# Loads of q and k by head group in a fused block-sparse attention and FFN kernel, with new instruction orders

## The chip, the cores and the metric

The kernel runs on one core of a Trainium2 chip. The metric is the device time of one execution in microseconds, the median of several runs. A profile is one execution recorded by the hardware profiler, with its own time. A core has the engines TensorE (PE), VectorE (DVE), ScalarE (ACT), GpSimd (POOL) and SyncE (SP); SP, ACT and POOL also issue DMAs, which 16 DMA engines carry out.

## The reference: what is computed

The inputs q, k and v have 4 batches, 8 heads, 768 positions and 64 dimensions, in float32. For every query, chunks of 32 keys are ranked by an upper bound of the score, the six best causal chunks are kept, and attention runs over them:

```python
k_chunks = k.reshape(B, H, nc, chunk, D)
k_min = np.min(k_chunks, axis=3)
k_max = np.max(k_chunks, axis=3)
ub = np.sum(np.maximum(q[:, :, :, None, :] * k_min[:, :, None, :, :], q[:, :, :, None, :] * k_max[:, :, None, :, :]), axis=-1)
ub = np.where(causal, ub, -1000000000.0)
top_chunks = np.argsort(ub, axis=-1)[..., -top_k:]
scores = scale * np.matmul(q, k.transpose(0, 1, 3, 2))
mask = sel & (pos[:, None] >= pos[None, :])
...
attn = attn / (np.sum(attn, axis=-1, keepdims=True) + 1e-09)
return np.matmul(attn, v).astype(np.float32)
```

The result, 3072 tokens by 512 features, goes through an RMS norm and a gated FFN:

```python
xn = x / rms * rms_g
g = xn @ w_gate
silu = g * (1.0 / (1.0 + np.exp(-g)))
return (silu * (xn @ w_val) @ w_out).astype(np.float32)
```

## The kernel before

**Blocks.** The tokens are cut into 12 blocks of 256, each a batch b and a third m of its sequence, in the order `ORDER` (line 340). Blocks 0, 1 and 2 of that order are (0,0), (1,0) and (2,0). The eight heads make two groups g of four heads a. In a tile with 128 partitions, partition 32a + r holds row r of head a.

**One block.** `load_qk` (line 423) issues the loads of q and k into `qraw` and `kraw`, `load_v` (451) those of v into `VX`, and `load_w` and `load_wo` those of the weights (`wg`, `wv`, `wo`, three pieces each). `job(i, g)` handles a group: VectorE transposes k and q in 32x32 squares (`turn k`, `turn q`, line 631), ACT or POOL casts them to bf16 (`half k`, `half q`), VectorE reduces the minima and maxima of the chunks (`ext0`, `ext1`), `dk` subtracts them, `bd0` and `bd1` lay them out for TensorE, and `relu` (725) takes the positive part of q over `qraw`. TensorE then forms the bounds (`upper`), VectorE makes the mask from them (`ubn`, `bar`, `top`, `mk`, `mt`, `swap`), TensorE computes the scores and adds the mask (`scores`, lines 751 and 762), ACT takes the exponential (`exp`, 801), POOL clears the triangle (`tri`, 771), TensorE multiplies by v (`values`, 827), and VectorE normalises (`rden`, `norm`). `norm` of a block (`square`, `rms`, `scale`, `turn`, `xsT`) is the RMS norm and the transpose for the FFN. The FFN has gate and value matmuls (`wg(i, tokens).h` and `wv(i, tokens).h`, line 951), an activation (`tanh`, `tg`, `vcopy`, `hh`) and the output projection (`project`, 998, which needs all of `wo`), then `out` and `store`.

**What sets the order.** Every operation is entered in a list with its readers and writers. `Plan.run` (227) then issues them in the order written in the table `STEPS`: entry e names operation e // 8 and, by e % 8, the engine that does it (0 PE, 1 ACT, 2 DVE, 3 POOL, 4 SP); a negative entry is a run of filler matmuls, which compute nothing that is used. `SLOTS` gives the buffer for each tile. Each engine does its instructions in this order and waits by semaphore for what it needs, so an operation also waits for all that stands ahead of it on its engine. The cost numbers in the code served the search for the order and do nothing at run time.

**Loads before.** In blocks 0 to 2 (`PACKED`) one DMA brings 32 rows of one head a for both groups, 128 KB, so k and q take four DMAs each. In block 0 they alternate between SP and ACT, in the others all are on SP. From block 3 on, a DMA brings one head of one group (64 KB). The first load of block 2 waits until the piece wg1 has landed, and the first of block 3 until wo0 has (`HELD`, 421). Weights and v are cast to bf16 on the way and come by POOL's queue. On POOL the order begins: constants, both v loads of block 0, wg0, `half k(0,0,0)`, wg1, `dk(0,0,0)`, wv0, wv1, both v loads of block 1, wg2, wv2, wo0, wo1, wo2, with small operations between them. On TensorE the first FFN matmul `wg(0,(0,)).0` stands ahead of `scores(1,0,1)0a` and `upper(1,0,1)`.

Of the kernel before, what the change touches and what calls it, by code (L numbers as in the profile page):

```python
# [33 lines left out]
class Plan:  # L34
# [213 lines left out]
def kernel(  # L248
# [113 lines left out]
    def dma(name, eng, src, dst, packets, cost, pri, writes, takes=(), reads=(), behind=()):  # L362
        occ = {"SP": 0.49 if pri < -400 else 0.57, "ACT": 0.46, "POOL": 0.78 if packets < 64 else 1.2}[eng]

        def start():
            o.inst = issuer[eng].dma_start(out=dst(), in_=src)  # L366
            for p in fences:
                tc.add_manual_dep(o.inst.ins, p.inst.ins.name, mybir.DependencyInfo(
                    mybir.DependencyClass.Sync, mybir.DependencyReason.DATA), reason="order")
# [727 lines left out]
```

## Time and profile before

| | us |
|---|---|
| median of 3 runs | 296.11 (295.57 to 296.67) |
| the profiled execution, its own time | 299.22 |
| span of the profiled execution | 297.2 |
| TensorE busy | 283.2 (95%) |
| VectorE busy | 222.1 (75%) |
| ScalarE busy | 207.7 (70%) |
| GpSimd busy | 164.8 (55%) |
| mean granted TensorE clock | 0.988 |

The page of a profile gives busy times, then the span in 40 equal slices with the busy share in tenths; in the DMA row this is the mean over the 16 DMA engines. A row of the timeline reads: start, duration, engine, line, operation, what it writes and reads, shapes and count; in brackets the idle time before it and what ended it. SPq, ACTq and POOL rows with DMA_DIRECT2D are the issues of DMAs. q1 is SP's queue, q10 ACT's and q0 POOL's. A row of the stage view gives the stretch, its length, TensorE's busy time and its count, the granted clock, the DMA share and GB/s. In the view of waits, a row is who waited for what: total, times, longest.

### The profile page before, as it was taken

What the parts mean: (1) busy time and instruction counts of PE and PEld (TensorE: products, weight loads), DVE (VectorE), ACT (ScalarE), POOL (GpSimd) and SP (SyncE); (2) the same over time, 40 slices, a digit from 0 to 9 for tenths busy, and PEclk for the clock granted to TensorE, in tenths of its full rate; (3) what the DMA queues carried; (4) which work ended last, traced back from release to release, by engine and by line L of the source; (5) the groups of instructions that cost most, each with busy time, mean ns of one, the idle gap of its engine ahead of it and who ended that gap; (6) DMA issues with size and microseconds to landing.
All of it is one profiled execution on the core that took longest, in us unless ns stands there. A gap on an engine that the chain in (4) does not pass through costs nothing.

```text
span 297.2 us, 11321 instructions
## 1 busy us (share of the span) xinstructions
PE 283.2 (95%) x4667; PEld 214.8 (72%) x4667; DVE 222.1 (75%) x633; ACT 207.7 (70%) x360; POOL 164.8 (55%) x259
## 2 busy tenths in 40 slices
PE   7796998999999999999999999999899999999995
PEld 7544897576867866888776787678668876688773
DVE  4785696899999899998979999978844643447141
ACT  2674786598797986898876797478596777564331
POOL 6985377969889887457593366209141253112510
PEclk9989799999999999999999999999999999999999
DMA  7999996955698877594979455202214001412012
GB/s 188 207 210 207 204 195 114 163 149 65 122 204 145 156 120 117 124 119 103 151 125 152 101 73 99 73 4 73 20 37 109 2 0 37 74 37 71 2 71 71
DMA packets 86387, 31.92 MB, mean 107 GB/s; under 512 B 74817, under 2 KB 81729, under 8 KB 86337
## 3 DMA queue, kind: packets, MB, share of 16 engines
q1 hardware_dynamic: 55776, 22.82, 33.5%
q0 software_dynamic: 29712, 7.87, 26.5%
q8 instruction: 36, 0.59, 0.9%
q10 hardware_dynamic: 848, 0.53, 0.8%
q14 instruction: 15, 0.11, 0.2%
HBM read 28.58 MB, written 6.29 MB: 117 GB/s over the span
## 4 chain that ended last, share of the span: by engine, by line
PE 60%; DVE 19%; DMA 7%; ACT 5%; POOL 4%; issue 3%; ACTq 0%; DVEq 0%
PE F L951 31%; PE F L998 15%; DMA VX<-in_v_dram 6%; PE F L827 5%; PE S L751 4%; DVE kx L646 3%; DVE m L576 2%; DVE tg L962 2%; ACT pt L801 2%; DVE qT L631 2%; PE S L762 2%; DVE mk L582 2%; DVE BD L473 2%; PE F L517 1%; DVE xnat L846 1%
## 5 line engine op out<-in xcount | busy, mean ns | idle before, releaser
L801 ACT ACTIVATE pt<-S 128x1024 bf16<-128x1024 f32 (+3 forms) x104 | 85.6, 861 | 32.7 <-PE S L762 27.6
L973 POOL TENSOR_TENSOR hh<-tg,vs 128x512 bf16<-128x512 bf16 x48 | 56.1, 1176 | 40.2 <-ACT vs L970 20.3
L951 PE MATMUL F<-xsT,wg 128*128 128x256 bf16 (+1 forms) x608 | 73.4, 268 | 1.9 <-DVE xnat L846 0.9
L962 DVE SCALAR_TENSOR_TENSOR tg<-th,F 128x512 bf16<-128x512 bf16 x72 | 48.1, 677 | 35.1 <-ACT th L958 33.8
L951 PE MATMUL F<-xsT,wv 128*128 128x256 bf16 (+1 forms) x608 | 73.3, 269 | 0.9 <-DVE tg L962 0.7
L998 PE MATMUL F<-wo,hh 128*128 128x512 bf16 (+1 forms) x300 | 68.8, 371 | 0.1
L951 PEld LDWEIGHTS <-wg 128*128 128x128 bf16 x608 | 55.6, 98 | 11.5 <-issue 2.3
L951 PEld LDWEIGHTS <-wv 128*128 128x128 bf16 x608 | 55.5, 98 | 10.4 <-issue 1.7
L771 POOL TENSOR_SCALAR_AFFINE_SELECT pt<-pt 128x512 bf16<-128x512 bf16 x48 | 31.9, 671 | 41.2 <-ACT pt L801 41.0
L958 ACT ACTIVATE th<-F 128x512 bf16<-128x512 f32 x72 | 42.7, 604 | 17.2 <-PE F L951 15.8
L998 PEld LDWEIGHTS <-hh 128*128 128x128 bf16 x300 | 27.9, 98 | 26.1 <-issue 1.2
L970 ACT ACTIVATE vs<-F 128x512 bf16<-128x512 f32 x48 | 28.2, 597 | 10.7 <-PE F L951 8.1
L751 PE MATMUL S<-qb,kb 32*128 32x256 bf16 (+1 forms) x800 | 32.8, 254 | 0.4 <-POOL kx L652 0.4
L646 DVE TENSOR_REDUCE kx<-kT 128x16 f32<-128x512 f32 x48 | 30.9, 669 | 0.0
L827 PE MATMUL F<-VX,pt 128*128 128x65 bf16 x672 | 27.5, 195 | 3.0 <-DMA VX<-in_v_dram 2.6
L827 PEld LDWEIGHTS <-pt 128*128 128x128 bf16 x672 | 25.5, 98 | 6.5 <-issue 2.9
L366 POOL DMA_DIRECT2D VX<-in_v_dram x24 | 22.9, 954 | 0.0
L751 PEld LDWEIGHTS <-kb 32*128 32x128 bf16 x800 | 13.6, 93 | 12.8 <-issue 11.4
L762 PE MATMUL S<-mtd,chunkrow 32*128 32x128 bf16 (+2 forms) x384 | 20.4, 204 | 0.0
L762 PE MATMUL S<-mto,chunkrow 32*128 32x128 bf16 (+2 forms) x384 | 19.8, 203 | 0.0
L846 DVE TENSOR_TENSOR xnat<-F,rden 128x256 bf16<-128x256 f32 x48 | 19.2, 412 | 0.7
L762 PEld LDWEIGHTS <-chunkrow 32*128 32x128 bf16 x768 | 18.6, 94 | 0.9
(72 smaller groups left out, 339.9 us busy)
## 6 DMA issues: line engine op xcount, KB each, us to landing
out_dram<-osb SPq DMA_DIRECT2D x23, 256.0 KB, 2.5
kraw<-in_k_dram SPq DMA_DIRECT2D x72, 64.0 KB, 3.1
qraw<-in_q_dram SPq DMA_DIRECT2D x72, 64.0 KB, 3.0
VX<-in_v_dram POOLq DMA_DIRECT2D x24, 128.0 KB, 5.0
QX<-qT SPq DMA_DIRECT2D x32, 64.0 KB, 2.9
wg<-in_moe_w_gate_dram POOLq DMA_DIRECT2D x3, 512.0 KB, 10.0
wv<-in_moe_w_val_dram POOLq DMA_DIRECT2D x3, 512.0 KB, 14.7
wo<-in_moe_w_out_dram POOLq DMA_DIRECT2D x3, 512.0 KB, 17.1
```

The costliest lines, as they stand in the source:

```text
L646: plan.op(f"ext{n}{J}", "DVE", 0.585, 0.67, lambda n=n, op=op: VE.tensor_reduce(out=at(kx)[:, g, n], in_=at(kT).rearrange("p h (j c x) -> ...
L751: TE.matmul(s[a // 2][:, a % 2, c0:c0 + q1 - q0], kbt[r, t, ks], qbt[r, t, q0:q1], start=(t == 0), stop=(t == 1 and not mask), skip_group_ ...
L762: TE.matmul(o, chunkrow[r, BLK * kg + P * e:BLK * kg + P * (e + 1)], mv, start=False, stop=(d == 1), skip_group_check=True)
L771: GE.affine_select(out=d, in_=d, compare_op=ALU.is_ge, fill=0.0, base=0, pattern=[[0, 4], [1, P]], channel_multiplier=-1)
L801: lambda pt=pt, hs=hs, c0=c0, c1=c1, x=sc[hp]: SE.activation(out=at(pt)[:, hs, c0:c1], in_=at(x)[:, :, c0:c1], func=ACT.Exp, scale=SCALE), ...
L827: TE.matmul(o[:, a, :], p_[:, a, off:off + P], vt[:, e, 4 * g + a, :], start=(kb_ == 0 and a == 0), stop=(kb_ == nkb - 1 and a == 3), skip ...
L951: TE.matmul(at(p_)[:, n * W:(n + 1) * W], w[:, g, ht * P:(ht + 1) * P], at(xT)[:, g, x0:x0 + W], start=(g == 0), stop=(g == NP - 1), skip_ ...
L958: plan.op(f"tanh{U}.{hp}", "ACT", 0.48, 0.6, lambda th=th, gp=gp: SE.activation(out=at(th), in_=at(gp), func=ACT.Tanh, scale=0.5), pri - 0 ...
L962: VE.scalar_tensor_tensor(out=at(tg), in0=at(th), scalar=1.0, in1=at(gp), op0=ALU.add, op1=ALU.mult), pri - 30, reads=[th, gp], writes=[tg ...
L970: plan.op(f"vcopy{U}.{hp}", "ACT", 0.48, 0.6, lambda vs=vs, vp=vp: SE.activation(out=at(vs), in_=at(vp), func=ACT.Copy), pri + 0.1, reads= ...
L973: plan.op(f"hh{U}.{hp}", "POOL", 1.11, 1.16, lambda tg=tg, vs=vs, hh=hh: GE.tensor_tensor(out=at(hh), in0=at(tg), in1=at(vs), op=ALU.mult) ...
L998: TE.matmul(at(op)[:, cs], at(key)[:, o:o + P], wo[:, ht, cs], start=(ht == 0), stop=(ht == NHT - 1), skip_group_check=True)
```

## The change

In blocks 0 to 2, one DMA brings one group: four heads of 32 rows, 256 KB, so k and q take two DMAs each. A transpose waits for the load of its own group. In block 0 the two k loads are on SP and the two q loads on ACT, behind the ACT table load. From block 3 on, a block's loads are the same DMAs in another order. `STEPS` and `SLOTS` are new throughout. The choice of engine differs for some 70 small operations, and `chunkrow` could be done by ACT but stays on VectorE. The load of rms_g no longer waits for a load of q, and `KX` no longer reads `kraw`.

In the new order SP begins with k of block 0 (group 0, 1), q of block 1 (0, 1), k of block 1 (0, 1), then k, q, q, k of block 2, and then block 3. POOL begins: constants (`eps` sixth among them), wg0, a v load of block 0, `half`, the other v load, wg1, wv0, two constants, both v loads of block 1, `dk(0,0,0)`, `relu(0,0,0)`, `bd1(0,0,0)`, `half k(0,0,0)`, wv1, ..., wg2, wv2, wo0, wo2, wo1. On TensorE the order is `upper(0,0,0)`, the scores and values of block 0, `upper(1,0,0)`, `scores(1,0,0)0a`, ..., `upper(1,0,1)`, `scores(1,0,1)0a`, and then `wg(0,(0,)).0`. There are 82 narrow and 20 wide fillers in place of 85 and 26. `wv(1,(0,1)).6` moves behind `project0.0`.

```diff
     STEPS = (
-        67, 228, 233, 3, 131, 27, 249, 244, 50, 260, 281, 34, 58, 9, 276, 265, 19, 99, 115, 139,
...
+        139, 228, 107, 27, 236, 131, 123, 50, 364, 3, 275, 9, 58, 241, 372, 249, 259, 348, 356, 19,
+        267, 34, 402, 291, 42, 418, 283, 426, 99, 115, 379, 458, 387, 474, 465, 490, 435, 547, 393,
...
-    def dma(name, eng, src, dst, packets, cost, pri, writes, takes=(), reads=(), behind=()):
...
+    def dma(name, engs, src, dst, packets, cost, pri, writes, takes=(), reads=(), behind=()):
+        engs = (engs,) if isinstance(engs, str) else engs
...
+        o = flex(name, {e: (occ[e], occ[e], start(e)) for e in engs}, pri,
+                 reads=list(reads) + list(behind), writes=writes, takes=takes)
...
+        flex("chunkrow", {"DVE": (2.2, 2.29, chunks(VE)), "ACT": (0.75, 0.84, chunks(SE))}, -300,
+             reads=["pat"], writes=["chunkrow"])
...
     def load_qk(i, nm, src):
         b, m = ORDER[i]
         key = (nm + "raw", b, m)
-        first = True
-        for n, a in enumerate((0, 2, 1, 3)):
-            eng = ("SP", "ACT")[n % 2] if i == 0 else "SP"
-            rows = slice(32 * a, 32 * (a + 1))
+        todo = []
+        for g in range(NG):
             if i in PACKED:
-                sv = src[b].rearrange("(g a) (m r j) d -> a m r g (j d)", a=4, m=NBLK, r=32)[a, m]
-                todo = [(sv, lambda rows=rows: at(key)[rows].rearrange("r g j h d -> r g (j h d)"),
...
+                sv = src[b].rearrange("(g a) (m r j) d -> g m a r (j d)", g=NG, m=NBLK, r=32)[g, m]
+                todo.append((g, sv, lambda g=g: at(key)[:, g].rearrange("p j h d -> p (j h d)"), 8, 0.104))
+                continue
+            for a in (0, 2, 1, 3):
+                rows = slice(32 * a, 32 * (a + 1))
+                sv = src[b, 4 * g + a, BLK * m:BLK * (m + 1), :].rearrange("(j r) d -> r j d", r=32)
...
+            dma(f"load {nm}{b}{m}{g}{n}", ("SP", "ACT") if i == 0 else ("SP",), sv, dst, packets, cost,
+                loads_due(i, nm == "q"), writes=[key + (g,)],
+                takes=[(key, nm + "raw")] if not n else (), reads=[key] if n else (),
+                behind=[HELD[i]] if i in HELD and not n else ())
...
-                    base + (0 if nm == "k" else 1) - first, reads=[raw] + ([T] if nm == "q" and g else []),
+                    base + (0 if nm == "k" else 1) - first, reads=[raw, raw + (g,)] + ([T] if nm == "q" and g else []),
...
-                    reads=[kx_, bd, kraw] + [kx_ + (x, "d") for x in range(NG)], writes=[bd, bd + (m_,)])
+                    reads=[kx_, bd] + [kx_ + (x, "d") for x in range(NG)], writes=[bd, bd + (m_,)])
...
-    plan.ops[-1].after.append([o for o in plan.ops if o.dma and o.name.startswith("load q00")][-1])
```

More of the change, by code (lines that the diff above doesn't have):

```diff
@@ L360, in due_ffn @@
         return PACE * i
-    def dma(name, eng, src, dst, packets, cost, pri, writes, takes=(), reads=(), behind=()):
[L363 to L369, printed above, removed]
-        fences = [p for key in behind for p in plan.wrote[key]]
-        o = plan.op(name, eng, occ, occ, start, pri,
-                    reads=list(reads) + list(behind), writes=writes, takes=takes)
-        o.dma = (packets, cost, eng != "POOL")
-        o.slack = MARGIN if pri > -30 and eng == "SP" else 0.0
-        return o
     def flex(name, alts, pri, **kw):
@@ L381, in flex, with start, go @@
         o.alts = alts
+        return o
+    def dma(name, engs, src, dst, packets, cost, pri, writes, takes=(), reads=(), behind=()):
+        engs = (engs,) if isinstance(engs, str) else engs
+        occ = {"SP": 0.57, "ACT": 0.46, "POOL": 0.78 if packets < 64 else 1.2}
+        def start(eng):
+            def go():
+                o.inst = issuer[eng].dma_start(out=dst(), in_=src)
+                for p in fences:
+                    tc.add_manual_dep(o.inst.ins, p.inst.ins.name, mybir.DependencyInfo(
+                        mybir.DependencyClass.Sync, mybir.DependencyReason.DATA), reason="order")
+            return go
+        fences = [p for key in behind for p in plan.wrote[key]]
+        o = flex(name, {e: (occ[e], occ[e], start(e)) for e in engs}, pri,
+                 reads=list(reads) + list(behind), writes=writes, takes=takes)
+        o.dma = (packets, cost, engs[0] != "POOL")
         return o
@@ L403, in constants, with chunks @@
             -378, reads=["ident"], writes=["pat"])
-        plan.op("chunkrow", "DVE", 0.8, 0.9, lambda: VE.tensor_scalar(
-            out=chunkrow.rearrange("p (c t) -> p c t", t=CH),
-            in0=pat[:, 0:S // CH].unsqueeze(2).to_broadcast([P, S // CH, CH]),
-            scalar1=MASKED, scalar2=None, op0=ALU.mult), -300, reads=["pat"], writes=["chunkrow"])
+        def chunks(eng):
+            out = chunkrow.rearrange("p (c t) -> p c t", t=CH)
+            x = pat[:, 0:S // CH].unsqueeze(2).to_broadcast([P, S // CH, CH])
+            if eng is SE:
+                return lambda: SE.activation(out=out, in_=x, func=ACT.Copy, scale=MASKED)
+            return lambda: eng.tensor_scalar(out=out, in0=x, scalar1=MASKED, scalar2=None, op0=ALU.mult)
+        flex("chunkrow", {"DVE": (2.2, 2.29, chunks(VE)), "ACT": (0.75, 0.84, chunks(SE))}, -300,
+             reads=["pat"], writes=["chunkrow"])
         for i, (key, t) in enumerate(BD.items()):
@@ L425, in load_qk @@
         key = (nm + "raw", b, m)
-        first = True
-        for n, a in enumerate((0, 2, 1, 3)):
-            eng = ("SP", "ACT")[n % 2] if i == 0 else "SP"
-            rows = slice(32 * a, 32 * (a + 1))
+        todo = []
+        for g in range(NG):
             if i in PACKED:
-                sv = src[b].rearrange("(g a) (m r j) d -> a m r g (j d)", a=4, m=NBLK, r=32)[a, m]
-                todo = [(sv, lambda rows=rows: at(key)[rows].rearrange("r g j h d -> r g (j h d)"),
-                         4, 0.104 if i == 0 else 0.12)]
-            else:
-                todo = []
-                for g in range(NG):
-                    sv = src[b, 4 * g + a, BLK * m:BLK * (m + 1), :].rearrange(
-                        "(j r) d -> r j d", r=32)
-                    todo.append((sv, lambda rows=rows, g=g: at(key)[rows, g].rearrange(
-                        "r j h d -> r j (h d)"), 16, 0.019))
-            for k_, (sv, dst, packets, cost) in enumerate(todo):
-                dma(f"load {nm}{b}{m}{a}{k_}", eng, sv, dst, packets, cost,
-                    loads_due(i, nm == "q"), writes=[key],
-                    takes=[(key, nm + "raw")] if first else (),
-                    behind=[HELD[i]] if i in HELD and first else ())
-                first = False
+                sv = src[b].rearrange("(g a) (m r j) d -> g m a r (j d)", g=NG, m=NBLK, r=32)[g, m]
[4 more added lines that the diff above has]
+                sv = src[b, 4 * g + a, BLK * m:BLK * (m + 1), :].rearrange("(j r) d -> r j d", r=32)
+                todo.append((g, sv, lambda rows=rows, g=g: at(key)[rows, g].rearrange(
+                    "r j h d -> r j (h d)"), 16, 0.019))
+        for n, (g, sv, dst, packets, cost) in enumerate(todo):
+            dma(f"load {nm}{b}{m}{g}{n}", ("SP", "ACT") if i == 0 else ("SP",), sv, dst, packets, cost,
+                loads_due(i, nm == "q"), writes=[key + (g,)],
+                takes=[(key, nm + "raw")] if not n else (), reads=[key] if n else (),
+                behind=[HELD[i]] if i in HELD and not n else ())
     def loads_due(i, n):
```

274 rows, old and new, of tables (SLOTS, STEPS) are left out of this document.

## The prediction

> **What bounds the kernel now.** I read the page first: its engine rows and its 40 slices.
>
> ```profile
> span 297.2 us, 11321 instructions
> PE 283.2 (95%) x4667; PEld 214.8 (72%) x4667; DVE 222.1 (75%) x633; ACT 207.7 (70%) x360; POOL 164.8 (55%) x259
> ...
> PE   7796998999999999999999999999899999999995
> ...
> DMA  7999996955698877594979455202214001412012
> ```
>
> TensorE is busy in nearly the whole span, with its gaps in the first four slices (7.43 us each), and there the DMA engines are full. What comes late in the first 30 us moves everything behind it; after that TensorE's own work sets the pace, beside a VectorE that is over 90% busy for much of 60 to 200 us. So I went on to the chain of work that ended last, and then to the time order of the first 55 us.
>
> ```profile
> 12.22 17.28 DMA VX<-in_v_dram
> ...
> 52.75 2.26 PE F L998 x10
> ```
> ```profile
> 4.98 0.71 DVE L631 STREAM_TRANSPOSE kT<-kraw 128x512 f32<-128x512 f32 x1 [2.20 <-DMA kraw<-in_k_dram]
> ...
> 9.41 0.29 PE L751 MATMUL S<-qb,kb 32*128 32x128 bf16 x8 [0.35 <-POOL kx L652]
> ...
> 19.77 0.70 DVE L631 STREAM_TRANSPOSE kT<-kraw 128x512 f32<-128x512 f32 x1
> ...
> 23.12 1.07 PE L951 MATMUL F<-xsT,wg 128*128 128x128 bf16 x16
> 24.12 0.29 PE L751 MATMUL S<-qb,kb 32*128 32x128 bf16 x8
> 24.34 0.39 PE L1066 MATMUL F<-chunkrow,ident 128*128 128x512 bf16 x1
> 24.66 0.44 PE L535 MATMUL F<-qT,BO 64*64 64x32 f32 x16
> 24.91 0.41 PE L535 MATMUL F<-qraw,BO 64*64 64x32 f32 x16
> ...
> 29.63 0.29 PE L827 MATMUL F<-VX,pt 128*128 128x65 bf16 x4 [2.42 <-DMA VX<-in_v_dram]
> ```
>
> The first transpose waits for k until 4.98; the first FFN matmul is at 23.12; TensorE then stands for 2.42 us for the second block's v, which is queued behind four 512 KB weight transfers on POOL's queue; the output projection starts near 52.7. All of it hangs on loads.
>
> **The change, part by part.**
>
> **The loads of q and k of blocks 0 to 2.** 24 DMAs of 128 KB (32 rows of one head, both groups) become 12 of 256 KB (one group, four heads). The bytes and the 2 KB runs stay. Issue time falls by 12 issues of some 0.44 us (two on SP take 0.87), worth nothing by itself, since both queues then stand idle.
>
> ```profile
> 0.80 0.87 SPq L366 DMA_DIRECT2D kraw<-in_k_dram  x2
> ...
> 1.73 0.45 ACTq L366 DMA_DIRECT2D qraw<-in_q_dram  x1
> ...
> 2.20 1.28 ACT L387 ACT_TABLE_LOAD   x1 [2.20 <-issue]
> 2.23 0.55 DVE L404 TENSOR_SCALAR chunkrow<-pat 128x768 bf16<-128x768 bf16 x1
> ...
> 4.34 2.00 POOL L366 DMA_DIRECT2D VX<-in_v_dram  x2
> ...
> 6.33 0.77 POOL L366 DMA_DIRECT2D wg<-in_moe_w_gate_dram  x1
> ...
> 7.33 1.11 POOL L639 CAST kb<-kT 128x512 bf16<-128x512 f32 x1
> ```
>
> What matters is how many of the 16 DMA engines carry one DMA.
>
> ```profile
> q10 hardware_dynamic: 848, 0.53, 0.8%
> ```
>
> ACT's queue q10 carries four row loads of 64 packets (256), the 512 four-byte elements of rms_g, and 80 more packets: 16 completions for each of its five DMAs. So each of the present loads is cut over all 16 engines. The row pattern of these loads begins with a count of 32. The new one begins with a count of 4: in memory the heads (a) lie a head apart and their 32 rows (r) lie a row apart, and the two can't be written as one count of 128. No row shows a DMA whose outermost count is not a multiple of 16, so the number of engines is unknown: 16 at best, and 4 (one per head) if the cut follows the outermost count. I take 4, because the number of engines must come from a count in the pattern, and 4 is the outermost in it; the first rival keeps 16. The Trainium skill, "DMA: Bandwidth & Descriptors", section "Why a DMA increments its semaphore by 16 and not by 1", states it as a rule: the engines of a DMA are the largest number up to 16 that divides the slowest dimension of both patterns, on SP's and ACT's queues the lowest-numbered ones. By that rule these loads run on the same four engines; by the present rows one would go on expecting 16. The q10 row agrees with it for counts of 32 and 128, and no run here yet shows it for 4.
>
> Price. Rates by stage, from the DMA view of three windows (1.8 to 6, 22 to 23, and 23.5 to 28.5 us):
>
> ```profile
> DMA packets 696, 1.15 MB, mean 275 GB/s; under 512 B 133, under 2 KB 133, under 8 KB 696
> ```
> ```profile
> DMA packets 293, 0.29 MB, mean 289 GB/s; under 512 B 124, under 2 KB 193, under 8 KB 293
> ...
> q1 hardware_dynamic: 119, 0.20, 62.4%
> q0 software_dynamic: 174, 0.08, 61.7%
> ```
> ```profile
> DMA packets 2038, 0.94 MB, mean 188 GB/s; under 512 B 1636, under 2 KB 1719, under 8 KB 2037
> ```
> ```profile
> GB/s 0 0 71 295 347 249 292 284 189 150 219 223 158 139 185 212 239 267 229 199 200 204 208 203 213 199 218 202 206 271 282 235 193 113 179 211 214 197 208 203
> ```
>
> The first is row loads alone; the second row loads beside weights, with equal busy shares for the two queues (62.4 and 61.7%); the third row loads beside v. The last line has the slices of the first 30 us, highest 347. Per engine that is 17.2, 18.1, 11.8 and at most 21.7 GB/s. The Trainium skill, same page, section "Queues, rings and completion order", says that an engine goes round its queues packet by packet; the equal shares agree.
>
> Blocks 0 and 1 have eight loads of 262 KB, 2.10 MB; on four engines 0.524 MB each. The weights and v that the new order has POOL issue before or during that (wg0, both v of block 0, wg1, wv0, both v of block 1, wv1: 2.62 MB) put another 0.164 MB on every engine. At 18.1 GB/s the 0.688 MB take 38.0 us. For the way to the first packet and from the last I add 2.5 us, which is what the 3.3 us from issue to landing of ACT's k loads leave beside their own transfer of some 0.8:
>
> ```profile
> kraw<-in_k_dram ACTq DMA_DIRECT2D x2, 128.0 KB, 3.3
> ```
>
> So the last k load of block 1, which is last in SP's order, lands at 40.5. Bounds: 26.7 with row loads always served first at 21.7; 45.5 at 16, between the mixed stages; and, on 16 engines, no later than now.
>
> **What waits for it.** In the new order `upper(1,0,1)`, which needs that load, stands ahead of the first FFN matmul `wg(0,(0,)).0` on TensorE (before, the FFN matmul came first). From the transpose of that k (19.77) to this upper (24.66) it takes 4.9 us now; the 15 VectorE instructions between them in the new order come to about the same (two reductions of 0.67, four norms of 0.41, nine small ones).
>
> ```profile
> L646 DVE TENSOR_REDUCE kx<-kT 128x16 f32<-128x512 f32 x48 | 30.9, 669 | 0.0
> L846 DVE TENSOR_TENSOR xnat<-F,rden 128x256 bf16<-128x256 f32 x48 | 19.2, 412 | 0.7
> ```
>
> With the upper (0.85, its two rows at 24.66 and 24.91) and the scores (0.29) the FFN starts 6.0 us after the landing: 46.5, against 23.12.
>
> From there to the first output projection it is 52.75 - 23.12 = 29.6 us now. Gone from this are the wait for v (2.42: v of block 1 is before wv1 in POOL's new order and lands before 40), the upper and scores already done (1.14), one filler (0.39), and one group of eight gate matmuls that moves behind the projection:
>
> ```profile
> 51.18 1.04 PE L951 MATMUL F<-xsT,wv 128*128 128x256 bf16 x8
> ```
>
> That leaves 24.6 and puts the projection at 71.1: 18.4 later, with 1.0 us of moved work to do, 19.4. I leave in this stretch the slow clock of 30.7 to 34.1, which followed the idle of 27 to 29.6; a longer idle ahead of the FFN brings the same.
>
> ```profile
> 30.00:32.00 2.00, 2.00 (x45) 0.67 1.21 200
> 32.00:34.00 2.00, 2.00 (x17) 0.50 1.25 207
> ```
>
> **POOL's order at the start.** wg0 goes ahead of v of block 0, and v of block 1 ahead of wv1, so seven DMA issues (0.77 for a weight, 1.0 for a v) stand ahead of `dk(0,0,0)`; before, it came after four. `half k(0,0,0)`, now behind `relu(0,0,0)`, then ends near 11.3 rather than 8.4, and the first scores come 2 us later than 9.41. On four engines that is hidden, since the second half of block 0's q lands near 20; on 16 it is the cost. `eps` and with it ACT's table load now precede ACT's two q loads: they issue near 2.6 instead of 1.7, hidden by the transposes of k. wg2, wv2 and wo stand behind the relu, bd and half of blocks 0 and 1 on POOL, so they too are issued 15 to 20 us later, and follow the shift of the FFN; what they cost beyond it I take as nothing and keep 5 us for the range.
>
> **SP.** Block 2's loads wait for wg1, as now, and block 3's for wo0; behind them stand only later loads and stores:
>
> ```profile
> SPq L366 <- DMA wo<-in_moe_w_out_dram: 16.1, 1, 16.1
> SPq L366 <- DMA wg<-in_moe_w_gate_dram: 10.1, 1, 10.1
> ```
>
> They shift with the weights. Eight more loads per block from block 3 on keep their form and change their order; nothing.
>
> **Engines exchanged.** Some 70 small operations change engine, and the three loads of VectorE, ACT and POOL hardly move. In the stretch where VectorE is full, four output copies leave it for ACT and two swaps and two QX copies come to it:
>
> ```profile
> L1016 DVE TENSOR_SCALAR osb<-F 128x512 f32<-128x512 f32 (+1 forms) x8 | 5.2, 652 | 5.3 <-PE F L998 5.2
> L592 DVE STREAM_TRANSPOSE mto<-mk 64x32 bf16<-64x32 bf16 (+1 forms) x10 | 3.0, 300 | 0.3
> L687 DVE COPY QX<-qT 128x512 f32<-128x512 f32 x1 | 0.4, 419 | 0.0
> ```
>
> Four times 0.65 leave; some 1.6 come (four halves of a swap at 0.30, a QX copy at 0.42). I take 1.0 as gain, between 0 and 2.6. For the rest of the new order, which fits longer loads better or worse than I can see, I take 0, within 3 either way.
>
> **Free edits.** `chunkrow` stays on VectorE and goes ahead of `own` (0.55 us in VectorE's 2.2 us wait for k). The dropped read of kraw by KX, the dropped wait of rms_g's load and the changed cost numbers add no instruction. Should the cover of VectorE's wait go, `chunkrow` costs 0.55. One filler group fewer: fillers run where TensorE waits.
>
> **Sum.** 19.4 - 1.0 = 18.4 later. The profiled execution took 299.22 us by its own time (span 297.2 and 2.0 around it); 317.6 for such an execution of the changed kernel. The median of the runs shown is 3.1 below it, 296.11, so 314.5; I say 314.
>
> **The rivals.**
>
> *The loads still run on 16 engines* (chance 0.12). For it speaks that every load in the profile does. Then one group's k is there about 1 us before the 4.98 of now, q and k of block 1 by 15, the wait for v (2.42) goes and with it most of the slow clock (some 1.5), and POOL's later `half k` costs about 1 of that, since 2 us at the first scores are partly caught up before the FFN: 3 us faster, 293. It decides if the first transpose of block 1's k starts before 22.
>
> *Four engines, but the row loads get most of them* (0.14). The landing at 26.7 to 32 puts the FFN start at 33 to 38 and the time at 301 to 306. Against it are the equal shares of the two queues.
>
> *Four engines, and the weights come last* (0.08). wo is issued behind block 1's work on POOL and shares the four engines with block 2's loads; the projection then waits beyond 71 for 8 us or more: 322 to 330. Against it: by then only 1 MB of row loads remains.
>
> *Sixteen engines and the gain given back in VectorE's full stretch* (0.04): 296.
>
> **How the numbers follow.** The forecast (four engines, landing between 32 and 45) has 0.62, and its own range is 304 to 322. Within 0.5% (1.5 us), about what a measurement of this kernel can tell from no change, lies the last rival and a little of the others, 0.05; faster, 0.12; slower, 0.83. A range from 298 to 324 holds the forecast, the second rival and a quarter of the third, and leaves out the 16-engine cases and the rest of the third: about 0.8.
>
> **What would show it.** Completion counts first: q10 now has 16 four-byte packets a DMA, and loads on four engines would have 4. Busy DMA shares in the first 40 us well below now, at GB/s near 70 to 150. The first transpose of k at 5.5 to 6.5, the second q transpose of block 0 near 20 and the last k transpose of block 1 near 41, each ended by a DMA. First FFN matmul near 46, projection near 71, and from there the same pace to the end. Wrong: a full DMA row in the first slices, or no wait for kraw after 10 us; then the 16-engine rival holds.

## The result, and the profile after

The changed kernel takes 319.28 us (318.42 to 319.6, four runs) against 296.39 us (295.57 to 297.48, four runs): a ratio of 1.0765, interval 1.0722 to 1.0808. It is 22.9 us slower.

The page of the changed kernel, with the lines that answer to those shown of before:

```profile
span 317.3 us, 11239 instructions
PE 282.1 (89%) x4621; PEld 216.9 (68%) x4656; DVE 221.0 (70%) x638; ACT 202.9 (64%) x346; POOL 169.4 (53%) x265
...
PE   7027797399999999989999999999999999999995
...
DMA  5993499459847788997876472342122202311003
...
q10 hardware_dynamic: 792, 0.53, 0.6%
```

TensorE's busy time is nearly the same (282.1 us against 283.2); what is new is idle time, 35.2 us of the span against 14.0, and nearly all that is new lies in the first eight slices, 63 us. In the DMA row the fourth and fifth slice (24 to 40 us) have a 3 and a 4, and the eighth and ninth (56 to 71 us) a 4 and a 5; before, the fourth to sixth had nines. The transfers are late although the DMA engines have time to spare. The last line gives the reason. ACT's queue has 256 row packets, 512 of rms_g and its 16 completions as before; of the 792 that leaves 8 for the two loads of q, four each. SP's queue agrees: it has 55496 packets against 55776, and the 280 are 16 completions for each of the 20 loads of before less 4 for each of the 10 that took their place. A four-head load runs on four DMA engines.

The chain of work that ended last names the two places where this is paid (start, duration, what):

```profile
3.86 24.38 DMA kraw<-in_k_dram
...
36.08 25.39 DMA kraw<-in_k_dram
63.42 1.87 PE F L952 x8
...
74.95 1.89 PE F L999 x8
```

Two waits for k, 24 and 25 us long, stand where before the chain had 17.28 us of v. The first is for block 1, the second for block 2. The time order on VectorE and TensorE shows what stands behind them:

```profile
6.90 0.71 DVE L632 STREAM_TRANSPOSE kT<-kraw 128x512 f32<-128x512 f32 x1 [4.02 <-DMA kraw<-in_k_dram]
...
16.54 0.71 DVE L632 STREAM_TRANSPOSE qT<-qraw 128x512 f32<-128x512 f32 x1 [7.62 <-DMA qraw<-in_q_dram]
...
31.85 0.71 DVE L632 STREAM_TRANSPOSE kT<-kraw 128x512 f32<-128x512 f32 x1
...
61.49 0.71 DVE L632 STREAM_TRANSPOSE kT<-kraw 128x512 f32<-128x512 f32 x1 [8.34 <-DMA kraw<-in_k_dram]
...
62.72 0.65 DVE L921 TENSOR_TENSOR xsT<-F,rmsg 128x512 bf16<-128x512 bf16 x1
```
```profile
38.38 1.36 PE L952 MATMUL F<-xsT,wg 128*128 128x128 bf16 x16
...
63.42 1.87 PE L952 MATMUL F<-xsT,wg 128*128 128x256 bf16 x8 [5.42 <-DVE xsT L921]
...
74.52 2.32 PE L999 MATMUL F<-wo,hh 128*128 128x512 bf16 x9
```

The first projection before:

```profile
52.68 2.33 PE L998 MATMUL F<-wo,hh 128*128 128x512 bf16 x10
```

The last k of block 1 is transposed at 31.85 (before 19.77), and 6.5 us later the first FFN matmul starts, at 38.38 (before 23.12). Then comes the second loss. `xsT`, which the FFN of blocks 0 and 1 needs, stands on VectorE behind the transpose of block 2's second k; that load lands at 61.4, `xsT` is made at 62.72, and TensorE has stood 5.42 us for it, after more idle time before. The first projection starts at 74.52 against 52.7. From there to the end of the span it takes 242.8 us; before, 244.5. So the start of the first projection, 21.8 us later, holds the whole 20.1 us between the two spans. The medians lie 22.9 us apart because the profiled execution of before took 2.8 us more than the median of its four runs.

Part of the loss is the clock behind the idle time, and no run prices it apart. The granted TensorE clock is 0.56 in 20 to 30 us and 0.66 in 60 to 70, where it was 1.00 before; the eight gate matmuls at 63.42 take 1.87 us, and eight of that shape took 1.04 before.

Why block 2 is so late is seen in SyncE's own rows (issues, then waits in total, times, longest):

```profile
3.86 30.96 SPq L374 DMA_DIRECT2D kraw<-in_k_dram  x3
34.87 1.10 SPq L374 DMA_DIRECT2D qraw<-in_q_dram  x2
```
```profile
SPq L374 <- DMA wg<-in_moe_w_gate_dram: 18.0, 1, 18.0
```

Before, block 2's loads began here:

```profile
18.37 0.78 SPq L366 DMA_DIRECT2D kraw<-in_k_dram  x2
```

The third load of the first row after the change is block 2's first. It waits 18.0 us for the weight piece wg1 (before 10.1) and goes out at 34.3 instead of 18.4. wg1 itself was issued at 4.8 us and took 29.4 us to land, against 10.0 before: four of the 16 engines are crowded with the row loads (in e4, where those of blocks 0 and 1 are spread over 16, it took 10.2). How the turns are shared is in the DMA view of 24 to 30 us:

```profile
DMA packets 527, 0.49 MB, mean 81 GB/s; under 512 B 303, under 2 KB 303, under 8 KB 527
...
q1 hardware_dynamic: 231, 0.46, 22.5%
q0 software_dynamic: 231, 0.03, 7.4%
```

SP's and POOL's queue get the same number of packets, 231, but SP's are 2 KB rows and POOL's are some 130 bytes of v: 0.46 MB against 0.03. The row loads run at 0.46 MB in 6 us, 77 GB/s, which is 19 GB/s on each of four engines and 22.5% of sixteen, while the other twelve have next to nothing to do. That an engine takes its queues in turn packet by packet is what the Trainium skill states, "DMA: Bandwidth & Descriptors", section "Queues, rings and completion order"; the equal counts agree. They are not seen everywhere: before, with row loads on 16 engines, SP's queue had 399 packets and POOL's 1638 in 23.5 to 28.5 us. Whether SP's queue had work on every engine then, the trace does not tell.

### The profile page after: what moved, and what is told of

Its sections match the earlier page's. It is cut to its first block, busy times and chain, and to the rows that moved or that the text cites. A ratio compares the mean times of both kernels' runs of the same rounds, so it can differ in the third digit from the quotient of the medians.

```text
span 317.3 us, 11239 instructions
## 1 busy us (share of the span) xinstructions
PE 282.1 (89%) x4621; PEld 216.9 (68%) x4656; DVE 221.0 (70%) x638; ACT 202.9 (64%) x346; POOL 169.4 (53%) x265
## 3 DMA queue, kind: packets, MB, share of 16 engines
q1 hardware_dynamic: 55496, 22.82, 28.7%
## 4 chain that ended last, share of the span: by engine, by line
PE 72%; DMA 17%; DVE 5%; issue 2%; ACT 1%; SPq 1%; POOL 0%; DVEq 0%; ACTq 0%
PE F L952 37%; PE F L999 18%; DMA kraw<-in_k_dram 16%; PE S L752 6%; PE F L828 5%; PE F L518 2%; PE S L763 2%; DMA xsT<-xs 1%; DVE kx L647 1%; PE F L536 1%; SPq L374 1%; DVE kT L632 1%; DVE tg L963 1%; ACT pt L802 1%; ACT th L959 1%
## 5 line engine op out<-in xcount | busy, mean ns | idle before, releaser
L974 POOL TENSOR_TENSOR hh<-tg,vs 128x512 bf16<-128x512 bf16 x48 | 56.9, 1193 | 53.3 <-ACT vs L971 22.9
L952 PE MATMUL F<-xsT,wg 128*128 128x256 bf16 (+1 forms) x608 | 75.0, 273 | 8.2 <-DVE xsT L921 7.7
L952 PE MATMUL F<-xsT,wv 128*128 128x256 bf16 (+1 forms) x608 | 75.1, 274 | 1.0 <-DMA xsT<-xs 0.8
L952 PEld LDWEIGHTS <-wg 128*128 128x128 bf16 x608 | 56.5, 100 | 17.5 <-issue 8.9
L999 PE MATMUL F<-wo,hh 128*128 128x512 bf16 (+1 forms) x269 | 65.1, 370 | 2.2 <-issue 0.5
L952 PEld LDWEIGHTS <-wv 128*128 128x128 bf16 x608 | 57.6, 101 | 11.1 <-issue 1.2
L959 ACT ACTIVATE th<-F 128x512 bf16<-128x512 f32 x72 | 42.6, 600 | 22.4 <-PE F L952 21.8
L971 ACT ACTIVATE vs<-F 128x512 bf16<-128x512 f32 x48 | 28.6, 601 | 18.4 <-PE F L952 16.6
L632 DVE STREAM_TRANSPOSE kT<-kraw 128x512 f32<-128x512 f32 x24 | 16.6, 696 | 14.8 <-DMA kraw<-in_k_dram 14.8
L632 DVE STREAM_TRANSPOSE qT<-qraw 128x512 f32<-128x512 f32 x24 | 16.5, 696 | 14.0 <-DMA qraw<-in_q_dram 13.9
L967 DVE TENSOR_TENSOR hh<-tg,F 128x512 bf16<-128x512 bf16 x24 | 16.2, 680 | 12.0 <-PE F L952 6.2
L752 PEld LDWEIGHTS <-kb 32*128 32x128 bf16 x800 | 13.7, 93 | 12.6 <-issue 11.6
```

The source lines that it names most:

```text
L632: lambda: VE.transpose(out=turned(nm).rearrange("p h (j r) -> p j h r", r=32, j=8), in_=at(raw)[:, g]),
L752: TE.matmul(s[a // 2][:, a % 2, c0:c0 + q1 - q0], kbt[r, t, ks], qbt[r, t, q0:q1], start=(t == 0), stop=(t == 1 and not mask), skip_group_ ...
L952: TE.matmul(at(p_)[:, n * W:(n + 1) * W], w[:, g, ht * P:(ht + 1) * P], at(xT)[:, g, x0:x0 + W], start=(g == 0), stop=(g == NP - 1), skip_ ...
L959: plan.op(f"tanh{U}.{hp}", "ACT", 0.48, 0.6, lambda th=th, gp=gp: SE.activation(out=at(th), in_=at(gp), func=ACT.Tanh, scale=0.5), pri - 0 ...
L971: plan.op(f"vcopy{U}.{hp}", "ACT", 0.48, 0.6, lambda vs=vs, vp=vp: SE.activation(out=at(vs), in_=at(vp), func=ACT.Copy), pri + 0.1, reads= ...
L974: plan.op(f"hh{U}.{hp}", "POOL", 1.11, 1.16, lambda tg=tg, vs=vs, hh=hh: GE.tensor_tensor(out=at(hh), in0=at(tg), in1=at(vs), op=ALU.mult) ...
```

## The experiments

Each ratio is against runs of the kernel before on the same chip (297.2 to 298.5 us in these, 296.39 for the result). Differences in us from the changed kernel are of medians, and the 1 to 2 us between these figures are in them. The profiled executions of e5 and e8 took 3.1 and 4.2 us more than their medians, so of them only the start is read.

### e2: the kernel before, with the new loads only

```diff
-                sv = src[b].rearrange("(g a) (m r j) d -> a m r g (j d)", a=4, m=NBLK, r=32)[a, m]
+                sv = src[b].rearrange("(g a) (m r j) d -> g m a r (j d)", a=4, m=NBLK, r=32)[n % 2, m]
...
+            if src is None:
+                return
```

> The kernel before, with its own order, where only the q and k loads of blocks 0 to 2 are made four heads of 32 rows by one group (two DMAs in place of the first two of four, nothing in place of the others). If the four engines are the cause, 310 to 325, with the last transposes of block 1's k beyond 28 us. If the new orders are the cause, within 2 us of 296.

318.94 us, 1.0700 (1.0619 to 1.0781): the changed kernel's time with none of its order. A piece of the chain that ended last, then the first FFN matmul and the first projection:

```profile
20.46 32.82 DMA VX<-in_v_dram
```
```profile
38.16 1.07 PE L953 MATMUL F<-xsT,wg 128*128 128x128 bf16 x16
...
72.33 2.33 PE L1000 MATMUL F<-wo,hh 128*128 128x512 bf16 x10
```

The load form alone is enough for the loss. The path is not the same: here the chain runs through block 1's v, which lands 32.8 us after its issue, and in the changed kernel through k. That the two orders come out alike, within the two intervals, is a result of the runs and not of one mechanism.

### e6: each new load cut in two loads of two heads

```diff
-                todo.append((g, sv, lambda g=g: at(key)[:, g].rearrange("p j h d -> p (j h d)"), 8, 0.104))
+                todo.append((g, [sv[2 * x:2 * x + 2] for x in range(2)], lambda g=g: [
+                    at(key)[64 * x:64 * (x + 1), g].rearrange("p j h d -> p (j h d)") for x in range(2)], 8, 0.104))
```

> The changed kernel with each four-head load cut into two loads of two heads (64 rows, 128 KB), 24 loads as in the run beside it. If the outermost count sets the engines, each runs on two: q10 shows 2 four-byte packets for each of its q loads (4 loads: 256 + 512 + 16 + 8 = 792 packets), the row loads move at some 38 GB/s in place of 76, block 1's last k lands beyond 55 us, and the time is 345 to 380. If the number of rows or the size sets them, it is within 5 us of the changed kernel's 319.

355.8 us, 1.1946 (1.1826 to 1.2065).

```profile
GB/s 104 168 41 41 42 99 40 63 199 122 79 96 105 128 74 155 158 154 129 150 150 90 153 118 94 152 61 128 21 32 19 82 41 2 53 55 85 9 0 119
...
q10 hardware_dynamic: 792, 0.53, 0.5%
```
```profile
61.03 0.71 DVE L635 STREAM_TRANSPOSE kT<-kraw 128x512 f32<-128x512 f32 x1
```

Smaller loads, twice as many, and 36 us more. In 18 to 44 us 41 GB/s come in, which is two engines at 20; the last k of block 1 is transposed at 61.03. The four loads of q again leave 8 packets of the 792 for their completions, now two each. So the count of engines follows the outermost count of the pattern, 2 here, 4 in the change, not the size and not the number of packets. This is the rule of the Trainium skill that the prediction weighed ("Why a DMA increments its semaphore by 16 and not by 1"): both values agree with it.

### e1, e3 and e4: sixteen engines for all three blocks, for block 2, for blocks 0 and 1

Each four-head load becomes four loads of 32 rows (64 KB, outermost count 32):

```diff
-                todo.append((g, sv, lambda g=g: at(key)[:, g].rearrange("p j h d -> p (j h d)"), 8, 0.104))
+                n = 4 if i in (0, 1, 2) else 1      # e3: (2,)   e4: (0, 1)
+                cuts = [slice(128 // n * x, 128 // n * (x + 1)) for x in range(n)]
+                todo.append((g, [sv[x] for x in range(4)] if n == 4 else [sv], lambda g=g, cuts=cuts: [
+                    at(key)[c, g].rearrange("p j h d -> p (j h d)") for c in cuts], 8, 0.104))
```

> The changed kernel with each four-head load issued as four loads of 32 rows (64 KB each, in place, same order of everything else), so that 16 engines carry each. If the four engines are the cause, the last k of block 1 is transposed before 20 us instead of at 31.85, the first FFN matmul is at 24 to 26 instead of 38.38, and the time falls to 291 to 296. If the new orders are the cause, it stays above 312.

> The changed kernel with 16 engines for block 2's loads alone. The first FFN matmul stays at 38 us; the wait for block 2's k at 61.49 goes. If block 2's loads cost what the two waits of TensorE behind xsT show (2.3 and 5.4 us) and the rest of that stretch, 307 to 312; if they are hidden, 318 to 320.

> The changed kernel with 16 engines for the loads of blocks 0 and 1 alone; block 2's stay on four. First FFN matmul at 24 to 26 us. Block 2's loads are issued once wg1 has landed, near 18 us, and take 1.05 MB at 75 GB/s, 14 us or more, so they land between 33 and 42. If the two stages add up, about 5 to 9 us above the first kernel of this group; if block 2's loads are hidden when they start early, within 2 us of it.

e1: 304.75 us, 1.0214 (1.0145 to 1.0284). e3: 307.7 us, 1.0317 (1.0247 to 1.0388). e4: 303.18 us, 1.0170 (1.0103 to 1.0236). First the rows of e3, then those of e4, then those of e1:

```profile
39.20 1.05 PE L957 MATMUL F<-xsT,wg 128*128 128x128 bf16 x16
...
61.90 2.32 PE L1004 MATMUL F<-wo,hh 128*128 128x512 bf16 x10
```
```profile
28.39 0.71 DVE L637 STREAM_TRANSPOSE kT<-kraw 128x512 f32<-128x512 f32 x1
...
36.18 1.05 PE L957 MATMUL F<-xsT,wg 128*128 128x128 bf16 x16
...
58.55 2.32 PE L1004 MATMUL F<-wo,hh 128*128 128x512 bf16 x10
```
```profile
0.80 3.92 SPq L376 DMA_DIRECT2D kraw<-in_k_dram  x8
...
4.76 8.35 SPq L376 DMA_DIRECT2D qraw<-in_q_dram  x8
...
6.64 10.77 ACTq L376 DMA_DIRECT2D qraw<-in_q_dram  x8
...
17.16 0.71 DVE L637 STREAM_TRANSPOSE qT<-qraw 128x512 f32<-128x512 f32 x1 [10.89 <-DMA qraw<-in_q_dram]
```

e3 leaves the first wait as it is (FFN at 39.20, 38.38 in the changed kernel) and takes the second away: from the FFN to the projection it takes 22.7 us instead of 36.1, and 11.6 us of the time are gone. e4 gains 16.1 us, and little of that at the first wait: its last k of block 1 is transposed at 28.39 and its first FFN matmul starts at 36.18, only 2.2 us earlier than in the changed kernel. Most of it is the second loss, which goes here too (22.4 us from the FFN to the projection). Where blocks 0 and 1 are on sixteen engines, wg1 lands early, block 2's loads go out at 22 us instead of 34.3 (e4), and four engines are enough for them. So the second loss is a consequence of the crowding in blocks 0 and 1, and e1, which has all three blocks on sixteen, gains no more than e4.

e1 missed what was expected of sixteen engines, 291 to 296 and an FFN start at 24 to 26; it starts at 36.43. Part of the reason is the experiment: blocks 0 and 1 now need 32 small loads, and SP issues eight without a break, the next eight only in 8.35 us as earlier ones land. ACT issues block 0's q from 6.64 to 17.41, as earlier loads land. e5 asks the same with fewer loads.

### e7: block 2's loads do not wait for wg1

```diff
-    HELD = {2:("wg",1),3:("wo",0)}
+    HELD = {3:("wo",0)}
```

> The changed kernel on four engines, where block 2's loads no longer wait for wg1. They follow block 1's on SP as soon as their buffers are free. If the wait for wg1 until 34.8 us is what makes block 2's k late at 61.5, it lands 10 us or more earlier and the time falls to 308 to 313. If the four engines' share is what counts, since weights then compete earlier, within 3 us of 319.

316.78 us, 1.0627 (1.0541 to 1.0714), 2.5 us below the changed kernel's median.

```profile
45.34 1.89 PE L952 MATMUL F<-xsT,wv 128*128 128x128 bf16 x16 [3.69 <-DMA wv<-in_moe_w_val_dram]
...
60.01 0.70 DVE L632 STREAM_TRANSPOSE kT<-kraw 128x512 f32<-128x512 f32 x1
...
71.29 2.32 PE L999 MATMUL F<-wo,hh 128*128 128x512 bf16 x10
```

Block 2's loads go out at 21 us instead of 35, and TensorE's wait for `xsT` is gone, but the projection starts only 3.2 us earlier: the loads now share the four engines with the weights that the FFN of blocks 0 and 1 needs, and TensorE stands 3.69 us for a piece of wv. The wait for wg1 is not what costs the 12 us; the four engines, which carry weights and rows together, are.

### e5: the new order with loads that use sixteen engines

Each new load is issued as two loads of the old form (one head for both groups, 128 KB), so there are 24 as before.

```diff
-                sv = src[b].rearrange("(g a) (m r j) d -> g m a r (j d)", g=NG, m=NBLK, r=32)[g, m]
-                todo.append((g, sv, lambda g=g: at(key)[:, g].rearrange("p j h d -> p (j h d)"), 8, 0.104))
+                sv = src[b].rearrange("(g a) (m r j) d -> a m r g (j d)", a=4, m=NBLK, r=32)
+                todo.append((g, [sv[x, m] for x in (2 * g, 2 * g + 1)], lambda g=g: [
+                    at(key)[32 * x:32 * (x + 1)].rearrange("r g j h d -> r g (j h d)") for x in (2 * g, 2 * g + 1)], 8, 0.104))
```

> The changed kernel with its order, where each of the twelve new loads is issued as two loads of the old form (32 rows of one head, both groups, 128 KB): 24 loads as before, on 16 engines, without the 48 issues and the long wait of ACT's q loads of the first run of this study. If that wait made the rest of that run's loss, q of block 0 is transposed before 10 us, the first FFN matmul is at 22 to 26 and the time 291 to 296. If the new orders are slower in themselves, it stays at 300 or more.

300.36 us, 1.0075 (1.0029 to 1.0120).

```profile
2.09 6.66 ACTq L376 DMA_DIRECT2D qraw<-in_q_dram  x4
...
15.59 0.71 DVE L635 STREAM_TRANSPOSE qT<-qraw 128x512 f32<-128x512 f32 x1 [7.66 <-DMA qraw<-in_q_dram]
...
32.60 1.66 PE L955 MATMUL F<-xsT,wg 128*128 128x128 bf16 x16
```

19 of the 23 us are back. But the new order on sixteen engines is no faster than the old one; it is slightly slower, and the first FFN matmul is at 32.60, not at 22 to 26. Block 0's q is transposed at 15.59; before, at 7.52:

```profile
7.52 1.29 DVE L631 STREAM_TRANSPOSE qT<-qraw 128x512 f32<-128x512 f32 x2
```

With e3 and e5 the loss divides, by the ratios: of the 7.65%, some 4.5 go when block 2 alone is on sixteen engines (e3), 2.4 more when blocks 0 and 1 are too and the loads are few (e5), and 0.75 stay.

### e8 to e12: where the order's own loss lies

Five variants of e5 try one cause each. e8 enters block 0's q loads ahead of block 1's q; e9 also issues block 1's k ahead of its q; e11 is e9 with the buffers of the new table put back (in e8 and e9, block 0's and block 1's q had exchanged theirs); e10 is e11 with POOL's first operations in the order of before; e12 is e11 with block 0's loads alternating between SP and ACT, ahead of the table load, as before.

```diff
-        139, 228, 107, 27, 236, 131, 123, 50, 364, 3, 275, 9, 58, 241, 372, 249, 259, 348, 356, 19,
+        139, 228, 107, 27, 236, 131, 123, 50, 3, 275, 9, 58, 241, 249, 364, 372, 259, 348, 356, 19,   # e8
+        139, 228, 107, 27, 236, 131, 123, 50, 3, 275, 9, 58, 241, 249, 348, 356, 259, 364, 372, 19,   # e9, e11
+        139, 228, 107, 27, 236, 131, 123, 50, 3, 9, 58, 241, 249, 348, 356, 259, 364, 372, 19, 267,   # e10
+        275, 34, 402, 411, 291, 42, 418, 426, 99, 115, 435, 283, 299, 458, 379, 387, 474, 465, 490,
+        139, 228, 107, 27, 236, 131, 123, 50, 3, 275, 58, 241, 249, 9, 348, 356, 259, 364, 372, 19,   # e12
...
+                    o.inst = issuer[("SP", "ACT")[n] if len(engs) > 1 else eng].dma_start(out=to, in_=x)   # e12
```

> The loads are those of the kernel before (two heads' worth of bytes over both groups, 128 KB, two for each new load), in the new order, and block 0's q loads are entered ahead of block 1's q loads; every engine and queue keeps its own order. Theory 1 (the new order loses because block 1's q loads take the places among the eight loads in flight that block 0's q needs): ACT issues its four q loads by 4.5 us instead of by 8.75, the first q of block 0 is transposed at 8 to 10 us instead of 15.59, the first FFN matmul starts at 24 to 29 instead of 32.60, and the time is 296 to 298, no more than 0.5% above the kernel before. Theory 2 (the order of the engines is slower by itself): the q transposes come earlier as well, but the time stays at 299.5 to 301.

> As the run with block 0's q first, and SP issues k of block 1 ahead of q of block 1, as in the kernel before. Block 1's k is transposed in this order of VectorE only behind block 1's q, so if the order of landing matters at all, theory 1 expects the same time within 1 us, 296 to 298, with the last k of block 1 transposed at 18 to 22 us (24.71 before the two edits). Theory 2: 299.5 to 301 as well.

> As the run with k of block 1 first, with its buffers put back to those of the new table, and POOL's order at the start as in the kernel before: both v loads of block 0 ahead of wg0, and half k(0,0,0), wg1 and dk(0,0,0) ahead of relu(0,0,0). Theory 1 (the new order loses its 2 us because weights come 4 us earlier and take two thirds and more of the DMA time from 5 to 8 us, which holds block 0's q and with it POOL's relu): the first q of block 0 is transposed at 10 to 12 us instead of 15.18, the first FFN matmul starts at 26 to 28 instead of 31.17, and the time is 296.5 to 298, no slower than the kernel before within 0.3%. Theory 2 (the order of VectorE, ScalarE and TensorE behind the start is slower by itself): q comes earlier as well, but the time stays 0.4 to 0.8% above the kernel before.

> As the run with k of block 1 first, with its buffers put back to those of the new table and nothing else, as the partner of the run with POOL's order. Since block 3's q then waits for block 0's q buffer and not for block 1's, it can only come earlier: 0 to 1 us below that run; first q of block 0 at 15, first FFN matmul at 31, 0.2 to 0.5% above the kernel before under both theories.

> As the run with the buffers put back, and block 0's four k and four q loads alternate between SP and ACT as in the kernel before, with ACT's table load behind them. Theory 1 (what is left of the loss comes from block 0's q, which on ACT alone, behind the table load and beside POOL's weights, lands at 14.7 us): all eight loads are issued by 2.7 us, the first q of block 0 is transposed at 8 to 10 us, the first FFN matmul starts at 24 to 28 instead of 30.39, and the time falls by 1 to 3 us against that run, to within 0.3% of the kernel before or below it. Theory 2 (the loss lies in the order of the engines behind the start): q comes as early, but the time stays 0.4 to 0.8% above the kernel before.

| | time, us | ratio to before | block 0's first q transposed | first FFN matmul | first projection |
|---|---|---|---|---|---|
| e5 | 300.36 | 1.0075 (1.0029 to 1.0120) | 15.59 | 32.60 | 56.40 |
| e8 | 299.43 | 1.0047 (1.0010 to 1.0084) | 14.82 | 30.71 | 53.15 |
| e9 | 299.66 | 1.0049 (1.0024 to 1.0075) | 15.18 | 31.17 | 54.61 |
| e11 | 299.44 | 1.0067 (1.0030 to 1.0105) | 14.71 | 30.39 | 52.82 |
| e10 | 301.63 | 1.0093 (1.0053 to 1.0133) | 13.85 | 31.73 | 55.90 |
| e12 | 300.2 | 1.0099 (1.0064 to 1.0135) | 8.43 | 30.16 | 52.59 |

In none of the runs that try a cause did the times come that were expected of it. With q issued by 7.0 instead of 8.75 (e8) it is transposed 0.8 us earlier, no more; that alone does not clear the limited number of loads under way, since 4.5 was expected, but in e12, where q is issued by 2.7, the time does not fall either. POOL's early weights are not either (e10 against e11: 0.9 us earlier at q, and no faster). e12 brings block 0's q as early as expected, and the FFN does not follow. VectorE in e12:

```profile
8.43 0.71 DVE L635 STREAM_TRANSPOSE qT<-qraw 128x512 f32<-128x512 f32 x1 [1.20 <-DMA qraw<-in_q_dram]
...
11.41 0.69 DVE L635 STREAM_TRANSPOSE qT<-qraw 128x512 f32<-128x512 f32 x1
17.79 0.71 DVE L635 STREAM_TRANSPOSE qT<-qraw 128x512 f32<-128x512 f32 x1 [5.68 <-DMA qraw<-in_q_dram]
18.42 0.13 DVE L656 TENSOR_TENSOR kx<-kx 128x16 f32<-128x16 f32 x1
18.48 0.30 DVE L564 STREAM_TRANSPOSE ubn<-F 128x32 f32<-128x32 f32 x2
```

At 11.41 block 0's last q is turned. Then VectorE stands 5.68 us for block 1's q, which the new order puts ahead of `ubn`, the mask of block 0. In e12 what comes earlier is caught there, and the first FFN matmul stays between 30 and 33 in all six. A late FFN start is not a late projection: in e12 it takes 22.4 us from one to the other, before 29.6. The wait is shown; that it makes the 0.5 to 1% is not. e11 and e12 reach the projection at 52.6 to 52.8, as the profile of before did (52.7), and that profile is of an execution 3 us above its median, so profiles do not tell where the rest lies. It stays open. None of these variants is faster than the kernel before.

## Why the prediction was right, and where it was not

314 us were predicted, with 304 to 322 as the forecast's own range; 319.28 came. The step that carried the forecast, **four engines for a load whose outermost count is 4**, was right, and the runs with counts of 2 and 32 show it from both sides. The sum came out near because two terms were wrong in opposite directions: the first FFN matmul came 8.1 us earlier than said, and the way from there to the projection was 11.5 us longer. That they nearly cancel is luck.

**The landing of block 1's last k** was put at 40.5 and was over by 31.85; the last row packets of SP's queue are in 31.0 to 31.5 us. That is outside the 32 to 45 of the forecast and inside the 26.7 to 32 of the second rival. The term that failed is the 0.164 MB of weights and v added to each of the four engines, as if queues had equal shares of time. In 24 to 30 us they had equal counts of packets, and the row loads took 0.46 of 0.49 MB. The rows alone, 0.524 MB per engine at the 18.1 GB/s of the prediction, take 29.0 us, with its 2.5 us at the ends 31.5, which is near the measured landing. This is the second rival's mechanism, which had 0.14, and the equal shares of time that I held against it (62.4 and 61.7%) were from a stage on all 16 engines in which POOL's packets had some 460 bytes (0.08 MB in 174).

**From the landing to the FFN** 6.0 us were predicted; from the last k transpose it was 6.5. The number holds, the path is not shown. The prediction put the wait on TensorE's order, with `upper(1,0,1)` ahead of the FFN. But e2 keeps the old order, with the FFN ahead, and starts it at 38.16. There `xsT` of block 0 is made at 37.30, behind the last k transpose of block 1 (34.82) on VectorE. In the changed kernel `xsT` is ready at 38.33, at the same time as the upper and the scores, so both paths end together there.

**From the FFN to the projection** 24.6 us were predicted and 36.1 came. The step that failed is the paragraph on SP with the last sentence on POOL: block 2's loads "shift with the weights", cost beyond it nothing, 5 us kept for the range. The weights that the row loads displaced are what releases block 2's loads, these then ran on four engines as well, and VectorE's `xsT` stood behind their transposes. e3, with block 2 alone on sixteen engines, has 22.7 us in this stretch, and its time is 11.6 us lower. The second rival stopped at 301 to 306 for the same omission; the third (weights last, 322 to 330) had the direction, though with wo, and not `xsT`, as what is waited for.

**Behind the projection** the pace was said to stay, and did: time less the start of the projection is 244.5 us for the profiled executions of the changed kernel (319.01 - 74.52) and 246.5 before (299.22 - 52.7). It is 244.6 in e3, 244.7 in e11 and 245.3 even in e6, whose projection starts at 110.1; and 246.5 in e2 and e12. So the pace is the same within 2 us, and these profiles do not tell whether the new order is shorter there.

**The median.** I took off 3.1 us because the profiled execution of before lay so far above its median. That was a property of that one execution: the profiled one of the changed kernel took 319.01, its median is 319.28. By its own time, 317.6 was predicted.

**The rest of the order at 0 within 3:** 0.5 to 1.0% slower on sixteen engines (e5, e8 to e12), 1.4 to 2.9 us, inside the bounds. On four engines the order changes the path and not the time (e2 and the changed kernel). **The first rival**, 16 engines and 293, would not have held even on 16 engines: it had the order as a gain of 3 us, and e5 is 0.75% slower. **The signs:** q10's packets were as said, and DMA shares and GB/s fell in the fourth and fifth slice; the first k transpose came at 6.90, not by 6.5, the first FFN matmul at 38.38, not 46, and the projection at 74.52, not 71. The last k transpose of block 1 came at 31.85, not near 41.

## What to carry to other kernels

Before merging loads into fewer and larger ones, look at the outermost count of the merged pattern, for in these runs it set how many DMA engines carried a load from SP or ACT: 256 KB with a count of 4 ran at 77 GB/s, and loads of 128 KB with a count of 2 at 41. A transfer confined to a few engines also delays those that are spread over all of them (wg1: 29.4 us to landing against 10.0); that they end with their slowest share is an inference, since the trace does not name a packet's engine. So follow what waits for the displaced transfers (here the weight that releases the next block's loads) and not only the load that was changed. In a kernel that runs at a steady pace behind its start, the time is the start of the steady part plus a constant (here 244.5 to 246.5 us), and experiments can be read from that one row to within such a spread.

## What the runs showed that was not expected

On the crowded engines two queues had equal numbers of packets in 24 to 30 us, 231 and 231, so 2 KB rows beside packets of some 130 bytes took 0.46 of 0.49 MB. And loads from SP and ACT have a limited number under way at once: in e1, SP's first eight take 3.92 us to issue, its next eight 8.35 and ACT's eight 10.77; in the first 30 us SP waits 12 times for an earlier load of q or k to land. What sets the number was not tried apart, nor whether it is the chip or the program. I had counted a DMA's issue at some 0.45 us and nothing else.
